# Query and key terms stored once in DRAM and repeated by the loads, with the projection chains in another order

## The chip, the cores and the metric

The kernel runs on one core of one Trainium2 chip. The metric is the device time of one execution in microseconds (us), as the median of several runs. The kernel before takes 1933.05 us (median of three runs, 1928.44 to 1935.05). The engines are called PE (TensorE, matmuls), PEld (its weight loads), DVE (VectorE), ACT (ScalarE), POOL (GpSimd) and SP (SyncE, which issues every DMA of this kernel). `L310` is line 310 of the kernel before, unless the text says that it is of the kernel after.

## The reference, cut to what matters

```
x: 2048 x 576;  q, k, v = x @ wq, x @ wk, x @ wv    (32 heads of 18, 4 segments of 512 positions)
for each segment s:
    p     = softmax(q_s k_s^T * 18**-0.5 + causal mask);   a_dot = p @ v_s
    a_mem = phi(q_s) M / (phi(q_s) z + 1e-6)               (phi(t) = t + 1 if t > 0 else exp(t))
    o_s   = g * a_mem + (1 - g) * a_dot                    (g = sigmoid(beta), one number a head)
    M, z += phi(k_s)^T v_s, sum of phi(k_s)
a = concat(o) @ wo
b = (silu(x @ w_gate) * (x @ w_up)) @ w_down               (hidden size 4608)
out = sg * a + (1 - sg) * b                                (sg = sigmoid of x . gate_w, one number a row)
```

All inputs and the output are f32. The kernel gets close to f32 by splitting each number into a high part and remainders, and multiplying the parts.

## The kernel before, in words

PE's program has three parts, one after the other in time.

**Part 1, the four segments (0 to 265 us).** A segment has nine *chains* and then eight *value steps*. A chain (`qk`, L301) is 14 matmuls (L127) into one PSUM bank and yields 128 rows of q or of k, transposed, for 512 positions; chain (m, u) is row block m of q (u = 0) or of k (u = 1), and chain (4, 0) holds the last 64 rows of both. The order is q0, k0, q1, k1, q2, k2, q3, k3, (4, 0). After the matmuls the bank is emptied: ACT copies the first bf16 term (L308), DVE takes the remainder `qr` (L309), ACT copies the second term (L318), POOL subtracts for the third (L319). The three terms stand in a tile `q3` of two buffers; `qr` has one. Where phi is wanted, ACT makes Relu and Exp of the bank (L316, L317) and DVE ends it (L321) into a tile `ph`. What a chain wants done besides is run in its middle (`mid`): in segment 0 the splitting of later weights (`q_split`, `v_split`, L104 on ACT and L105 on DVE).

The stores of q3 to DRAM (`stk`) are put on a list and issued by `flush` (L297 to L299), at a chain all but one (all but four at the last). A value step (`v_step`, L339) is 14 matmuls (L127, with `vw`) for 128 positions and half of the heads, into one of three banks. ACT copies the result to f32 (L347) and to the first bf16 term (L348), DVE takes the remainder (L349), ACT and POOL make the second and third term (L352, L353). In the segments after the first a memory step (L417) follows each value step, and during the chains the state M is brought up to date with the last segment's k and v: transposes of phi(k) (L379, L382), their copy `kt` (L380, L383, L384), matmuls L371. Before each value step `flush()` issues every store that is left; then, step by step, one of five loads of x for the next segment (`x_load`, L170) is issued, and split a step later (L104, L105, and L142, L143 for the fifth).

The stack in DRAM is `stk[2, 4, 576, 6, 512]`: for each row of q and of k six bf16 rows. For q these are high, middle, low, high, middle, high; for k low, middle, high, middle, high, high. So the 108 rows of one head (18 times 6) multiply to the six products of q and k parts that matter. A chain's stores write three of the six; DMAs from DRAM to DRAM (`copies`, L329) write the other three: four a segment after value steps 1 to 4 (L543), and for the last segment sixteen smaller ones during the feed-forward (L943).

**Part 2, feed-forward and attention together (265 to about 1820 us).** The 36 column blocks f of the hidden layer are run for one half of the positions and then for the other, 72 times eight *ticks*. Each tick is one group of matmuls (L910, L916), and `beat` adds down-projection groups (L758) and steps of the attention (`att_gen`, L689). In the first half each f loads raw weights (`raw`, L196), makes seven operands out of them and stores those (`wc`, L239; `rc`, L242); in the second half it loads them again (`w_fetch`, L562 and L566) as soon as PE has freed a buffer. Down-projection weights are loaded in the first half (`draw`, L201), split (L850, L851), stored (`dc`, L740), and fetched in the second (`dw`, L745).

The attention goes by *units*: 64 units, each two heads of one segment, five steps a unit. The maxima of a unit are found first (`s_bank`, L595), its probabilities later (`t_bank`, L635). Unit u has two tiles out of four, `qst` and `kst`, each [128, 2 heads, 512]; `stack_load` (L178, issues L182) fills their 108 rows by two DMAs, one for q and one for k, both heads at once. It is called at step 2 of the unit before (L700). Row maxima go to DRAM at step 3 (L696, which waits for POOL) and come back as three more rows of `qst` at step 0 of the next unit (`row_load`, L185).

**Part 3 (from about 1820 us)** is the output projection.

The order of every engine's instructions is written out by hand (manual schedule): each engine takes them in that order, and SP too, so a DMA whose data or buffer is not ready holds up all DMAs behind it. A DMA counts on one of eight semaphores in turn, and so also waits for the one that used its semaphore before.

Of the kernel before, what the change touches and what calls it, by code (L numbers as in the profile page):

```python
# [12 lines left out]
F32 = mybir.dt.float32  # L13
# [42 lines left out]
def gated_mix(ctx, tc, xT, wf, wd, wv, wo, beta, cmask, ident, bmask, out):  # L56
# [108 lines left out]
    def staging():  # L165
        return x_slot(*next(turns), F32).rearrange("p a b -> p (a b)")
# [92 lines left out]
    with ExitStack() as st:  # L259
# [22 lines left out]

        def v_load(hf):
            n = 288 + 2 * hf
            for a, b in ((0, 3), (3, 5)):
                raws["v", hf, a] = staging()[:, :(b - a) * n].rearrange("p (k n) -> p k n", n=n)
                nc.sync.dma_start(raws["v", hf, a], wv[:, a:b, 288 * hf:288 * hf + n])

        def v_split(hf):
            n = 288 + 2 * hf  # L290
            for a, b in ((0, 3), (3, 5)):
                split(vw[hf][:, 0, a:b, :n], vw[hf][:, 1, a:b, :n], raws["v", hf, a])

# [7 lines left out]
        def qk(s, m, u, mid=()):  # L301
            t = chain_tile()
            hi, lo = qw[m]
            products(t, w_stat(hi[:, u], lo[:, u]), x_side(*xs_of[s]))
            q3 = sp.tile([P, 3, L], BF, name="q3")
            qr = sp.tile([P, L], F32, name="qr", bufs=1)
            z0, z2 = (2, 0) if u else (0, 2)
            nc.scalar.activation(q3[:, z0], t, AF.Copy)  # L308
            nc.vector.tensor_sub(qr, t, q3[:, z0])  # L309
# [9 lines left out]
            nc.gpsimd.tensor_sub(q3[:, z2], qr, q3[:, 1])  # L319
            if ph is not None:  # L320
                nc.vector.scalar_tensor_tensor(ph, t, 0.0, ph, op0=OP.max, op1=OP.add)  # L321
            if m < 4:
                late.append((stk[u, s, m * P:m * P + P, 0:3], q3))
            else:
                late.append((stk[0, s, 512:D, 0:3], q3[0:64]))
                for z in range(3):
                    late.append((stk[1, s, 512:D, 2 - z], q3[64:128, z]))

        def copies(s, n=1):  # L329
            r = []  # L330
            for kind in range(2):
                for c, m in ((3, 2), (5, 1)):
                    z = 3 - m if kind else 0
                    for i in range(n):
                        a, b = D // n * i, D // n * (i + 1)
                        r.append((stk[kind, s, a:b, c:c + m], stk[kind, s, a:b, z:z + m]))
            return r

        def v_step(s, hf, i):  # L339
# [91 lines left out]
        for kt in range(NT):  # L431
# [4 lines left out]
            xr.append(raw)  # L436
        q_load(0, 1)
        nc.vector.memset(vf[:, :, :, DH:E], 1.0)
# [6 lines left out]
        for kt in range(NT):  # L445
            x_split(xs_of[0], kt, xr[kt])
        q_load(1, 0)
        q_load(1, 1)
        q_split(0, 1)
        q_split(1, 0)  # L450

        def small():
            nc.sync.dma_start(idt, ident)
            nc.sync.dma_start(bg, bass.AP(tensor=beta.tensor, offset=beta.offset, ap=[[0, P], [1, H]]))
            nc.scalar.activation(bg, bg, AF.Exp, scale=-1.0)
# [9 lines left out]

        loads = {0: [lambda: q_load(2, 0), lambda: q_load(2, 1)], 1: [lambda: q_load(3, 0), lambda: q_load(3, 1)],
                 2: [lambda: q_load(4, 0)], 4: [lambda: v_load(0)], 5: [lambda: v_load(1)], 7: [small]}
        def x_first():
# [18 lines left out]

        chains = [(m, u) for m in range(5) for u in range(2 if m < 4 else 1)]
        for s in range(NSEG):
            upd = upd_gen(s - 1) if s else None  # L490
            casts = []
            for n, (m, u) in enumerate(chains):
                mid = []
                if s == 0:
                    for z in loads.get(n, []):
                        z()
                    if n + 3 < 9:
                        mid.append(lambda n=n: q_split(*chains[n + 3]))
                    if n in (6, 7):
                        mid.append(lambda n=n: v_split(n - 6))  # L500
                if s == 1 and n < 3:
                    cast = masks(*((0, 3), (3, NT), (0, 0))[n])
                    casts.append(cast)
                if s == 1 and 3 <= n < 6:
                    mid.append(casts[n - 3])
                qk(s, m, u, mid)
# [11 lines left out]
            for n in range(8):  # L518
# [5 lines left out]
                if s < 3:  # L524
                    if n == 0:
                        xs_of[s + 1] = x_tiles(s + 1)
                    if n < 5:
                        raws["x", n] = x_load(s + 1, n)
                    if 1 <= n < 6:
                        x_split(xs_of[s + 1], n - 1, raws["x", n - 1])  # L530
                else:
# [7 lines left out]
                    for _ in range((0, 0, 0, 0, 3, 3, 6, 6)[n]):  # L539
                        if start[0][0] < 8:  # L540
                            start.pop(0)[1]()
                if 0 < n < 5 and s < 3:
                    nc.sync.dma_start(*copies(s)[n - 1])  # L543
        flush()


    with ExitStack() as st:
# [37 lines left out]
        stack_load(0)  # L585
        SPLAN = [[(0, 0, 3)], [(0, 1, 3)], [(384, 0, 0), (0, 0, 2)], [(384, 1, 0), (0, 1, 2)], [(0, 0, 1), (256, 1, 1)]]
# [102 lines left out]
        def att_gen():  # L689
            N = 10 * NB  # L690
            for tau in range(N + TL + VL + 4):
# [230 lines left out]
        for pos, (half, f) in enumerate(seq):  # L922
# [178 lines left out]
```

## Time and profile before

| what | before |
|---|---|
| median of three runs | 1933.05 us (1928.44 to 1935.05) |
| the profiled execution | 1932.2 us |
| its span, first to last instruction | 1930.4 us |
| PE busy | 1836.8 us (95%) |
| mean granted PE clock | 0.986 |
| DMA packets | 213860, 344.94 MB |
| segments start, on PE | 5.18, 65.03, 130.89, 201.01 us |
| their value steps start | 37.03, 106.06, 173.70, 242.64 us |
| first feed-forward matmul | 265.25 us |
| first s_bank of unit 0, of unit 32 | 292.7, 1109.4 us |

The profile is of one execution. Its *windows* give the busy time of each engine in a stretch, its *timeline* the instructions in order with the idle time before each and, behind an arrow, what ended that idle time; its *waits* sum these by line. Busy time of PE is that of pipelined matmuls, so a high share isn't full use, but idle time is idle.

### The profile page before, as it was taken

The page shows a single profiled execution, that of the slowest core. Times are in us where ns is not written, and L with a number is a line of the kernel's source. Part 1 is how long each engine was busy: PE and PEld are TensorE (multiplying, and loading weights), DVE is VectorE, ACT ScalarE, POOL GpSimd, SP SyncE. Part 2 cuts the span into 40 slices and gives each one's busy share as a digit, 9 for nine tenths or more (in the row PEclk, how much of TensorE's full clock was granted, in tenths as well). Part 3 has the DMA queues.
Part 4 walks back from the last instruction along what each step waited for, and adds up shares of the span by engine and source line. Part 5 has one row for each costly group of instructions (what it writes and reads, how often), then busy time and mean ns, then how long its engine had stood idle before and what let it go on. Part 6 is the DMA issues. An engine that isn't in the chain of part 4 may idle for free.

```text
span 1930.4 us, 35822 instructions
## 1 busy us (share of the span) xinstructions
PE 1836.8 (95%) x12508; PEld 1555.5 (81%) x12508; DVE 1229.5 (64%) x3032; ACT 965.2 (50%) x1800; POOL 857.6 (44%) x1246
## 2 busy tenths in 40 slices
PE   8888989999999999999998999999999999999999
PEld 6777878788788778877887788788888878888899
DVE  5354377767777787778767655656555666555355
ACT  6445454555664565566545545444544444455211
POOL 2222262345455555555554544544445444445121
PEclk9999989999999999999999999999999999999999
DMA  5553467745764674566456636544654465455544
GB/s 188 199 206 114 167 229 269 243 143 190 236 208 154 211 237 152 176 222 238 134 176 225 224 114 178 179 135 124 192 162 140 136 194 151 117 164 153 176 153 141
DMA packets 213860, 344.94 MB, mean 179 GB/s; under 512 B 37872, under 2 KB 100720, under 8 KB 213680
## 3 DMA queue, kind: packets, MB, share of 16 engines
q1 hardware_dynamic: 213680, 342.65, 54.5%
q8 instruction: 99, 1.62, 0.4%
q14 instruction: 81, 0.66, 0.1%
HBM read 208.49 MB, written 148.24 MB: 185 GB/s over the span
## 4 chain that ended last, share of the span: by engine, by line
PE 65%; DVE 8%; ACT 5%; DMA 4%; issue 3%; POOL 1%; SPq 0%; DVEq 0%; ACTq 0%; POOLq 0%
PE bank L910 25%; PE bank L758 23%; PE bank L916 4%; PE bank L635 3%; PE bank L595 3%; PE bank L127 3%; PE bank L664 2%; PE bank L666 1%; DMA raw<-in_wf_dram 1%; ACT L639 1%; DMA stk<-stk 1%; DVE p L712 1%; DMA woraw<-in_wo_dram 1%; ACT pe L639 1%; DVE hl L851 1%
## 5 line engine op out<-in xcount | busy, mean ns | idle before, releaser
L714 POOL TENSOR_TENSOR p<-pe,p 128x512 f16<-128x512 f32 x320 | 372.8, 1165 | 685.3 <-DVE p L712 603.5
L758 PE MATMUL bank<-dw,hh 128*128 128x288 f32 x2304 | 484.0, 303 | 16.4 <-DVE ya L763 11.9
L758 PEld LDWEIGHTS bank<-dw,hh 128*128 128x128 f32 x2304 | 379.9, 189 | 39.4 <-DVE ya L763 19.0
L639 ACT ACTIVATE pe<-bank 128x512 f32<-128x512 f32 x320 | 191.0, 597 | 340.7 <-PE bank L635 299.8
L758 PE MATMUL bank<-dw,hl 128*128 128x288 f32 x1152 | 341.2, 296 | 2.1 <-DVE hl L105 2.1
L763 DVE TENSOR_TENSOR ya<-bank,ya 128x288 f32<-128x288 f32 x352 | 159.9, 456 | 229.1 <-PE bank L758 227.0
L602 DVE CUSTOM_DVE_ANT_0 scr<-bank,cm 128x512 bf16<-128x512 f32 (+3 forms) x512 | 247.2, 483 | 15.6 <-PE bank L595 8.7
L758 PEld LDWEIGHTS bank<-dw,hl 128*128 128x128 f32 x1152 | 217.9, 189 | 2.5 <-DVE hl L105 2.5
L635 PE MATMUL bank<-qst,kst 111*128 111x512 bf16 (+3 forms) x512 | 151.8, 305 | 0.0
L712 DVE CAST p<-pe 128x512 f16<-128x512 f32 x320 | 151.0, 472 | 1.0 <-POOL pe L647 0.9
L647 POOL TENSOR_SCALAR_AFFINE_SELECT pe<-pe 128x256 f32<-128x256 f32 (+1 forms) x320 | 135.2, 422 | 11.2 <-ACT pe L639 10.2
L595 PE MATMUL bank<-kst,qst 108*128 108x512 bf16 (+3 forms) x512 | 126.3, 300 | 11.7 <-ACT pe L639 11.7
L993 DVE TENSOR_TENSOR bank<-bank,row 128x512 f32<-128x512 f32 x72 | 50.3, 699 | 106.0 <-ACT row L989 105.4
L980 ACT ACTIVATE row<-bank 128x512 f32<-128x512 f32 x72 | 43.0, 597 | 134.7 <-PE bank L916 134.0
L639 ACT ACT_TABLE_LOAD x66 | 84.7, 1283 | 46.3 <-PE bank L635 45.4
L105 DVE TENSOR_TENSOR hl<-row,hh 128x512 fp32r<-128x512 f32 x72 | 51.8, 720 | 76.4 <-ACT hh L104 76.4
L127 PE MATMUL bank<-xo,qhi 128*128 128x512 f32 x288 | 94.8, 410 | 5.3 <-ACT xo L104 5.2
L319 POOL TENSOR_TENSOR q<-qr,q 128x512 bf16<-128x512 f32 x36 | 42.3, 1175 | 118.6 <-ACT q L318 107.5
L635 PEld LDWEIGHTS <-kst 111*128 111x128 bf16 x512 | 47.9, 97 | 51.1 <-issue 35.9
L984 ACT ACTIVATE bank<-bank 128x512 f32<-128x512 f32 x72 | 41.9, 582 | 90.8 <-PE bank L910 87.2
L986 ACT ACT_TABLE_LOAD x67 | 86.0, 1283 | 1.2
L969 ACT ACTIVATE bank<-bank 128x512 f32<-128x512 f32 x72 | 42.0, 583 | 81.6 <-PE bank L910 71.5
(2083 smaller groups left out, 4286.9 us busy)
## 6 DMA issues: line engine op xcount, KB each, us to landing
raw<-in_wf_dram SPq DMA_DIRECT2D x72, 320.0 KB
dc<-dw SPq DMA_DIRECT2D x36, 576.0 KB
dw<-dc SPq DMA_DIRECT2D x36, 576.0 KB
qst<-stk SPq DMA_DIRECT2D x64, 216.0 KB
kst<-stk SPq DMA_DIRECT2D x64, 216.0 KB
stk<-q SPq DMA_DIRECT2D x32, 384.0 KB
draw<-in_wd_dram SPq DMA_DIRECT2D x36, 288.0 KB
vd<-vps SPq DMA_DIRECT2D x8, 912.0 KB
```

The lines of the kernel that those rows point to most:

```text
L127: nc.tensor.matmul(t, st[n], mv[n], start=(n == 0), stop=(n == 13))
L595: nc.tensor.matmul(t[:, c:c + w], qs[:KR, pr, P * i:P * i + P], ks[:KR, pr, 0:w], start=True, stop=True)
L602: nc.vector.tensor_tensor_reduce(scr[:, :w], t[:, c:c + w], cm[:, L - w:L], 1.0, -3.0e38, OP.add, OP.max, m[:, k:k + 1])
L635: nc.tensor.matmul(t[:, c:c + w], ks[:KR + 3, pr, P * j:P * j + P], qs[:KR + 3, pr, P * j:L], start=True, stop=True)
L639: nc.scalar.activation(pe, t, AF.Exp, scale=SCALE)
L647: nc.gpsimd.affine_select(d, d, pattern=pat, compare_op=OP.is_ge, fill=0.0, base=0, channel_multiplier=-1)
L712: nc.vector.tensor_copy(p1, pe)
L714: nc.gpsimd.tensor_sub(p2, pe, p1)
L758: nc.tensor.matmul(t, p, q[:, cs], start=(n == 0), stop=(n == 3 * CH - 1))
L763: nc.vector.tensor_add(ya[:, i, cs], t, ya[:, i, cs])
L910: nc.tensor.matmul(t, w[:, p, z], x[z][:, q], start=first and n == 0, stop=last and n == 5, skip_group_check=True)
L986: nc.scalar.activation(sg0, sg0, AF.Silu)
```

## The change

The stack in DRAM has three rows for each row of q or k, high, middle, low for both. A chain stores three terms at once, the last chain 64 rows to each of q and k; the copies from DRAM to DRAM are gone. `stack_load` now makes the six: for q the high rows three times over, the middle twice and the low once (a leading step of zero repeats the source), for k high, middle, low, then high, middle, then high. This takes ten DMAs a unit in place of two: six at step 2 (head 0's four, and the last 18 rows of q and of k for both heads) and four at step 3 (head 1), behind that step's store of maxima.

The chains go q0 to q3, (4, 0), k0 to k3. `q3` has four buffers and `qr` two, the phi of k one in place of two. `flush` keeps two stores back at every chain. The loads of x for the next segment are issued ahead of the last chains (segment 0: two, two and one ahead of chains 6, 7, 8; segments 1 and 2: one ahead of each of chains 4 to 8) and no more in the value steps. In segment 0 the splits of the value weights are spread over chains 3, 6, 7, 8, the f32 copy of the values is made by DVE and not by ACT, and the constants of beta are computed in segment 1's chain 7. The order of PE's instructions, by shapes and tiles, is that of before.

```diff
-    stk = dram.tile([2, NSEG, D, 6, L], BF, name="stk")
+    stk = dram.tile([2, NSEG, D, 3, L], BF, name="stk")
...
-    def stack_load(u):
+    def stack_load(u, pr):
         s, b = divmod(u, 16)
-        for kind, t in ((0, qst), (1, kst)):
-            src = stk[kind, s, 2 * b * DH:2 * b * DH + 2 * DH]
-            nc.sync.dma_start(t[u % NST][0:KR], src.rearrange("(j r) c n -> (r c) j n", r=DH))
+        q, k = (stk[kind, s, 2 * b * DH:2 * b * DH + 2 * DH].rearrange("(j r) z n -> r j z n", r=DH)
+                for kind in range(2))
+        tq, tk = qst[u % NST], kst[u % NST]
+        for z, n in ((0, 3), (1, 2)):
+            r0 = (0, 3 * DH)[z]
+            qz = q[:, pr, z]
+            nc.sync.dma_start(tq[r0:r0 + n * DH, pr],
+                              bass.AP(tensor=qz.tensor, offset=qz.offset, ap=[[0, n]] + list(qz.ap)))
+            nc.sync.dma_start(tk[r0:r0 + n * DH, pr], k[:, pr, 0:n].rearrange("r z n -> z r n"))
+        if pr == 0:
+            nc.sync.dma_start(tq[5 * DH:KR], q[:, :, 2])
+            nc.sync.dma_start(tk[5 * DH:KR], k[:, :, 0])
...
-            q3 = sp.tile([P, 3, L], BF, name="q3")
-            qr = sp.tile([P, L], F32, name="qr", bufs=1)
+            q3 = sp.tile([P, 3, L], BF, name="q3", bufs=4)
+            qr = sp.tile([P, L], F32, name="qr")
...
-                ph = sp.tile([P, L], F32, name=f"ph{m}{u}", bufs=2 if u or m == 4 else 1)
+                ph = sp.tile([P, L], F32, name=f"ph{m}{u}", bufs=2 if m == 4 else 1)
...
-            nc.scalar.activation(fv, pv, AF.Copy)
+            if s:
+                nc.scalar.activation(fv, pv, AF.Copy)
+            else:
+                nc.vector.tensor_copy(fv, pv)
...
+        chains = [(m, 0) for m in range(NT)] + [(m, 1) for m in range(4)]
...
-        chains = [(m, u) for m in range(5) for u in range(2 if m < 4 else 1)]
...
+                if s < 3:
+                    for kt in ((0, 1), (2, 3), (4,))[n - 6] if s == 0 and n > 5 else (n - 4,) if s and n > 3 else ():
+                        raws["x", kt] = x_load(s + 1, kt)
                 qk(s, m, u, mid)
-                flush(4 if m == 4 else 1)
+                flush(2)
...
-                    if n < 5:
-                        raws["x", n] = x_load(s + 1, n)
...
-                if 0 < n < 5 and s < 3:
-                    nc.sync.dma_start(*copies(s)[n - 1])
...
-                if n == 2 and u + 1 < 2 * NB:
-                    stack_load(u + 1)
+                if n in (2, 3) and u + 1 < 2 * NB:
+                    stack_load(u + 1, n - 2)
...
-            if half == 0 and 4 <= f < 20:
-                defer(4, lambda f=f: nc.sync.dma_start(*copies(NSEG - 1, 4)[f - 4]))
```

More of the change, by code (lines that the diff above doesn't have):

```diff
@@ L281, in q_split, with v_load, v_split @@
             split(qw[m][0][:, u], qw[m][1][:, u], raws[m, u])
-        def v_load(hf):
+        def v_load(hf, a, b):
             n = 288 + 2 * hf
[L285 to L289, printed above, removed]
+            raws["v", hf, a] = staging()[:, :(b - a) * n].rearrange("p (k n) -> p k n", n=n)
+            nc.sync.dma_start(raws["v", hf, a], wv[:, a:b, 288 * hf:288 * hf + n])
+        def v_split(hf, a, b):
             n = 288 + 2 * hf
-            for a, b in ((0, 3), (3, 5)):
-                split(vw[hf][:, 0, a:b, :n], vw[hf][:, 1, a:b, :n], raws["v", hf, a])
+            split(vw[hf][:, 0, a:b, :n], vw[hf][:, 1, a:b, :n], raws["v", hf, a])
         late = []
@@ L322, in qk @@
             if m < 4:
-                late.append((stk[u, s, m * P:m * P + P, 0:3], q3))
+                late.append((stk[u, s, m * P:m * P + P], q3))
             else:
[L325 to L337, printed above, removed]
+                for kind in range(2):
+                    late.append((stk[kind, s, 512:D], q3[64 * kind:64 * kind + 64]))
         def v_step(s, hf, i):
@@ L436, in gated_mix @@
             xr.append(raw)
-        q_load(0, 1)
+        chains = [(m, 0) for m in range(NT)] + [(m, 1) for m in range(4)]
+        q_load(*chains[1])
         nc.vector.memset(vf[:, :, :, DH:E], 1.0)
@@ L446, in gated_mix @@
             x_split(xs_of[0], kt, xr[kt])
[L447 to L450, printed above, removed]
+        q_load(*chains[2])
+        q_load(*chains[3])
+        q_split(*chains[1])
+        q_split(*chains[2])
         def small():
@@ L454, in small, with betas @@
             nc.sync.dma_start(bg, bass.AP(tensor=beta.tensor, offset=beta.offset, ap=[[0, P], [1, H]]))
+        def betas():
             nc.scalar.activation(bg, bg, AF.Exp, scale=-1.0)
@@ L498, in gated_mix @@
                         mid.append(lambda n=n: q_split(*chains[n + 3]))
-                    if n in (6, 7):
-                        mid.append(lambda n=n: v_split(n - 6))
+                    if n in halves:
+                        mid.append(lambda n=n: v_split(*halves[n]))
                 if s == 1 and n < 3:
@@ L584, in gated_mix @@
             nc.gpsimd.memset(mbs[i], 0.0)
-        stack_load(0)
+        for pr in range(2):
+            stack_load(0, pr)
         SPLAN = [[(0, 0, 3)], [(0, 1, 3)], [(384, 0, 0), (0, 0, 2)], [(384, 1, 0), (0, 1, 2)], [(0, 0, 1), (256, 1, 1)]]
```

17 lines of the change are left out of this document (11 added, 6 removed).

## The prediction

> **What bounds the kernel now.** I read first the page's busy shares, then the windows by stage. The program's first part (L127 projections, four segments of the sequence) ends at 265.25 us, where the first feed-forward matmul (L910) starts; feed-forward and attention fill the rest.
>
> ```profile
> PE 1836.8 (95%) x12508; PEld 1555.5 (81%) x12508; DVE 1229.5 (64%) x3032; ACT 965.2 (50%) x1800; POOL 857.6 (44%) x1246
> ```
>
> ```profile
> 0.00:65.03 65.03, 51.27 (x238) 43.83 (x239) 29.98 (x48) 38.12 (x70) 17.71 (x26) 0.93 0.64 220
> 65.03:130.89 65.86, 57.96 (x347) 51.52 (x347) 28.51 (x75) 34.10 (x70) 17.76 (x21) 1.00 0.48 172
> 130.89:201.01 70.12, 60.75 (x349) 54.18 (x348) 30.70 (x83) 34.22 (x70) 18.42 (x22) 0.95 0.46 165
> 201.01:265.25 64.24, 59.35 (x349) 52.90 (x348) 32.02 (x82) 32.33 (x67) 27.43 (x28) 0.97 0.47 173
> 265.25:292.70 27.45, 20.33 (x66) 14.58 (x65) 19.46 (x42) 15.39 (x37) 16.12 (x19) 0.69 0.64 225
> 292.70:1109.40 816.70, 783.78 (x5283) 652.51 (x5283) 613.79 (x1480) 462.00 (x908) 411.47 (x591) 0.99 0.60 201
> 1109.40:1782.50 673.10, 663.63 (x4912) 554.44 (x4911) 400.41 (x1079) 318.86 (x513) 321.98 (x508) 1.00 0.52 153
> ```
>
> Each row: stretch, length, busy time of PE, PEld, DVE, ACT, POOL, then granted clock, DMA share, GB/s. From 292.7 us on PE is busy 96 to 99%: nothing there can be won by moving loads. The four segments leave PE idle 36 of 265 us. PE's, ACT's and SP's timelines of the first segment say why.
>
> ```profile
> 46.75 3.25 PE L127 MATMUL bank<-vw,xo 128*128 128x288 f32 x12 [3.98 <-DVE r L349]
> 54.15 1.87 PE L127 MATMUL bank<-vw,xo 128*128 128x290 f32 x12 [1.09 <-DVE r L349]
> 61.82 2.93 PE L127 MATMUL bank<-vw,xo 128*128 128x290 f32 x12 [3.31 <-DVE gl L351]
> ```
>
> ```profile
> 34.51 0.60 ACT L308 ACTIVATE q<-bank 128x512 bf16<-128x512 f32 x1 [2.06 <-DMA stk<-q]
> ...
> 52.31 0.63 ACT L104 ACTIVATE xo<-xo 128x512 fp32r<-128x512 f32 x1 [3.54 <-DMA xo<-in_xT_dram]
> ...
> 59.81 0.63 ACT L104 ACTIVATE xo<-xo 128x512 fp32r<-128x512 f32 x1 [3.02 <-DMA xo<-in_xT_dram]
> ```
>
> ```profile
> 38.73 10.55 SPq L299 DMA_DIRECT2D stk<-q x6
> 49.38 1.03 SPq L170 DMA_DIRECT2D xo<-in_xT_dram x2
> 50.50 0.53 SPq L543 DMA_DIRECT2D stk<-stk x1
> ```
>
> PE waits for PSUM banks that ACT and DVE have not emptied. ACT is late twice: in the chains it waits for a store to free one of two q3 buffers, and in the value steps for x loads. Those stand on SP behind the stores of the last chains, and on the rings behind the 576 and 1152 KB copies. The same x waits come in segment 1 (ACT: 4.60, 1.51, 4.25 us) and segment 2 (4.81, 1.55, 4.64); the last makes the first state update of the next segment late (L371 waits 2.91, 3.96, 2.77 us for ACT's kt). After such waits the trace's clock records show half speed (6.8 us from 45.1, 3.4 us each at 62.2, 147.5, 191.9, 215.8).
>
> **The change, part by part.** PE's instruction list keeps shapes and order, so only waits move.
>
> *Segment 0.* Chains stay at 31.85 us: their loads keep their lead, and ACT per chain is at most copy 0.60, split 0.66 to 0.95, Relu and Exp 1.23, second copy 0.61, some 3.2 us against PE's 3.18. The 28.0 us of value steps (37.03 to 65.03) become eight times 1.87 (PE's step where nothing waits) plus 1 for ACT's lag: 16. ACT's step falls to 0.41 + 0.46 + 0.61 and a 0.5 wait for DVE, below 2.0, since the vf copy (0.39) goes to DVE, which has 0.46 + 0.46 + 0.69 a step. The x loads, issued from chain 6 on (26 us), take 5 to 10 us and are there at 37. Gain **12**.
>
> *Segments 1 and 2.* Segment 1's chains take 41.03 - 1.46 - 2.91 = 36.7 without waits, its value steps 24.83 - 2.92 - 0.61 = 21.3. I leave 0.5 for the kt wait (ACT needs 4.4 us from a chain's end to kt, PE comes after 4.0) and 0.2 more: 58.7 each, against 65.86 and 70.12. Gains **7.2** and **11.4** (in segment 2 two spells of half clock go too).
>
> *Segment 3.* Chains 41.63 become 37.2; its value steps lose only L417's 0.45 us wait. Gain **4.8**. The transition (265 to 293) waits on feed-forward operands being made (L229) and keeps its length.
>
> At nothing: the second head's loads move past the maxima store, which waits for POOL (L696, 89.1 us in all); from that store to their first use were 9.7 us or more. The 28 copies leave SP (0.49 to 0.63 us each) and the rings; where they ran in the feed-forward PE did not wait for them. One buffer for each k phi is enough, as the transposes end at chain 4 and the first k chain is 5; if they ran late, ACT would wait for one of them (0.3 us). The gate constants move to segment 1's chain 7, ahead of their first reader. The late stores keep two behind: with four q3 buffers a store may take 12.7 us after its chain, and POOL (about 5), issue and landing need some 8.
>
> *Ten stack loads for two.* This costs. SP: 8 more issues a unit. The nearest rows are the old stack load (0.36 and 0.41) and the v fetch (L189, 0.54, whose two sides differ in form as these do); I take 0.54, near 4.5 us a unit of 19.8 in the second half. Behind them on SP stand weight fetches (L562), maxima (L696) and row loads (L185). Each DMA also waits for the one eight before it, through eight semaphores. Rings: in the trace an old stack load of 108 rows ends with 13 completion marks, the 8-row maxima store with 9, the 3-row load with 4, every 128-row one with 16; so few rows use few engines, one for each mark but one. The new loads lead with 3 and 2 on the DRAM side and I expect 4 and 3 marks. A 1 KB packet takes 46 ns (median). If all use the same engines, the two busiest get 8 x 18 + 2 x 4 = 152 packets a unit, 7.0 us, against 36 and 1.7 before. The second half's DMA share of 0.52, less the old stack loads' 0.06, is 0.46 of other traffic; 7.0 of 19.8 us is 0.35 more: 0.81, not full. A load right behind the first head's six is issued 4 x 0.6 + 2 x 0.45 - 0.8 = 2.5 us later than before and finds about 1 us more on the ring: 3.5 us later; behind all ten, some 5.
>
> [...]
>
> Who waits? I paired landings with first uses. Old stack loads land 3.8 us or more before use, median 10. Weight fetches of the second half: 24 of 312 have under 5 us, and 5 us on every one would come 18.6 us short in all; about a third stand behind a burst: 5 us. Of 36 down-weight loads (L201), 24 are short-notice; 13 of these have under 3.5 us; a quarter stand behind a burst, some 1.8 us short each, half of it on PE: 3 us. Bounds: nothing (slack takes all) and 60 us (every weight fetch 6 us late comes 58.8 short). I take **8**, near the lower end, since a burst lasts 3 to 6 us and most slack is longer; the first unit's ten loads, issued near 280 us with 7.5 us of slack before, are in it.
>
> Sum: -12 - 7.2 - 11.4 - 4.8 + 8 = -27.4 on the profiled execution's 1932.2 us (span 1930.4 and 1.8 around it): 1904.8. The median of the runs is 0.85 above that execution: **1905.7**.
>
> **The rivals.**
>
> *Nothing paid later* (1898): slack hides all bursts. For: no matmul has waited more than 0.5 us in all for a stack load. Against: 0.02 to 3.5 us slack of many L201 loads.
>
> *Half the gain* (1923): x comes early, but the kt waits (L371, 9.6 us) and the L417 waits (7.7) are ACT's and DVE's own and stay: 17.3 less. For: ACT's 4.4 us from chain to kt is already more than PE's 4.0. Against: segment 3's value steps, with operand splits but no x loads, run at 22.6 for 21.2.
>
> *The narrow loads take over* (slower, 1950): weight fetches of the second half land later than their slack. The shortfalls summed over all fetches pass 41 us (the gain and the 0.3%) when each is 5.6 us later; at 6 they are 59. With 59 the sum is 1933 - 35.4 + 59 = 1957; I put it at 1950, some stalls covering others. For: 0.81 is a mean, and stretches at 0.69 DMA share (275 to 350) reach 0.95; two bursts within 3 us, in about 13 of the second half's units, make 11 DMAs in a row. Against: the first-half fetch slack is 11 us or more (L196), and a fetch far behind a burst loses nothing.
>
> That the chains' reorder does nothing by itself is part of the second rival.
>
> **How the numbers follow.** Forecast 0.55, nothing paid 0.17, half the gain 0.14, narrow loads take over 0.14. Within 0.3% of 1933 (1927 to 1939, about what a measurement of this kernel can tell from no change) I see 0.05, from the seams of the last two; faster by more 0.84, slower 0.11. The range leaves out most of the last rival: 1893 (no tax and 4 us more from the clock) to 1930 (tax of 32).
>
> **What would show it.** Right: the first L910 near 230 us; no ACT wait for in_xT in segments 1 to 3; L371 and L417 waits near 1 us; stack loads with 4 and 3 marks, issue about 0.5 us. Tax: PE waits in the feed-forward for L201's ACT copy, for wo from DMA, or for kst; their sum is to be near 8. Wrong: the first L910 after 245, or PE's waits for DMA over 30.

## The result, and the profile after

The changed kernel takes **1913.1 us** (median of four runs, 1911.2 to 1916.0), beside 1932.65 us of the kernel before on the same chip: a ratio of 0.9902, with a 95% interval of 0.988 to 0.9925. That is 19.6 us faster. The forecast was 1905.7, 7.4 us too low. The profiled execution took 1915.99 us (span 1914.2), the highest of its four. In this part line numbers are those of the kernel that the fence is from; L917, L602 and L369 of the changed kernel are the old L910, L595 and L371.

The page of the changed kernel has this line of busy times. PE does the same 12508 matmuls. Its busy time is nearly the same in sum, but the windows below show that this is two shifts that cancel.

```profile
PE 1834.5 (96%) x12508; PEld 1552.9 (81%) x12508; DVE 1231.5 (64%) x3040; ACT 965.6 (50%) x1792; POOL 858.2 (45%) x1246
```

The windows of the changed kernel, cut at the same instructions as those of before (four segments, the transition to unit 0's first maxima, the rest of the first half, most of the second half); the columns are as in the prediction.

```profile
0.00:54.12 54.12, 46.45 (x238) 40.00 (x239) 31.26 (x49) 35.88 (x61) 17.07 (x25) 1.00 0.63 217
54.12:115.60 61.48, 58.54 (x348) 52.62 (x347) 33.17 (x90) 36.96 (x77) 19.18 (x22) 0.97 0.38 134
115.60:173.32 57.72, 57.09 (x349) 51.41 (x348) 30.85 (x83) 34.47 (x71) 18.50 (x22) 1.00 0.38 138
173.32:231.12 57.80, 57.13 (x349) 51.40 (x348) 29.83 (x75) 31.00 (x62) 26.73 (x27) 1.00 0.46 169
231.12:263.10 31.98, 19.62 (x66) 13.62 (x64) 19.70 (x42) 15.51 (x37) 16.09 (x19) 0.77 0.52 185
263.10:1091.65 828.55, 790.30 (x5283) 656.87 (x5282) 610.61 (x1480) 462.19 (x908) 410.89 (x591) 0.98 0.58 193
1091.65:1766.38 674.73, 664.33 (x4912) 554.19 (x4911) 401.28 (x1079) 319.31 (x513) 322.50 (x508) 1.00 0.50 155
```

Set beside the old lengths, each row is a term of the prediction's sum:

| stretch | before | after | gain | predicted |
|---|---|---|---|---|
| segment 0 | 65.03 | 54.12 | 10.9 | 12 |
| segment 1 | 65.86 | 61.48 | 4.4 | 7.2 |
| segment 2 | 70.12 | 57.72 | 12.4 | 11.4 |
| segment 3 | 64.24 | 57.80 | 6.4 | 4.8 |
| transition | 27.45 | 31.98 | -4.5 | |
| first half after it | 816.70 | 828.55 | -11.9 | |
| second half | 673.10 | 674.73 | -1.6 | |
| end | 147.90 | 147.82 | 0.1 | |
| transition to end | 1665.15 | 1683.08 | -17.9 | -8 |

Part 1 gained 34.1 of the 35.4 us forecast. The tax on the rest was 17.9 us in this execution and not 8: 11.9 in the first half, 4.5 in the transition, 1.6 in the second half. By medians the tax is about 34.1 - 19.6 = 14.5 us, an estimate that takes part 1 to be as long in the other executions (this one was 2.9 us above the median).

Not all of this is waiting. In part 1 PE's busy time falls from 229.3 to 219.2 us and its idle time from 35.9 to 11.9: 24.0 of the 34.1 us are waits, and 10.1 are matmuls that take less time. Before, the clock records show half speed for 20.5 us of part 1, in five spells; now for 3.4 us, in one. In the first half it is the other way round: busy 790.30 us for 783.78, so 6.5 of the 11.9 us are longer matmuls and 5.3 are waits.

In segments 2 and 3 PE is idle 0.63 and 0.67 us now (length less busy time). Segments 0 and 1 show what stayed. This is PE's timeline of the changed kernel; the bracket is the idle time before the instruction and what ended it.

```profile
45.64 1.85 PE L127 MATMUL bank<-vw,xo 128*128 128x290 f32 x12 [0.19 <-DVE r L347]
48.88 1.85 PE L127 MATMUL bank<-vw,xo 128*128 128x290 f32 x12 [1.11 <-DVE r L347]
52.16 1.85 PE L127 MATMUL bank<-vw,xo 128*128 128x290 f32 x12 [1.17 <-DVE gl L349]
...
67.69 2.52 PE L369 MATMUL bank<-vf,kt 128*128 128x152 f32 x9 [2.89 <-ACT kt L378]
```

ACT's and DVE's timelines of the same stretch give the reason: ACT hardly waits for x loads any more (0.4 us in all), but for DVE.

```profile
44.51 0.43 ACT L346 ACTIVATE vps<-bank 128x288 bf16<-128x288 f32 x1 [1.25 <-DVE vf L345]
45.53 0.46 ACT L350 ACTIVATE vps<-r 128x288 bf16<-128x288 f32 x1 [0.59 <-DVE r L347]
45.88 0.61 ACT L104 ACTIVATE xo<-xo 128x512 fp32r<-128x512 f32 x1
47.74 0.43 ACT L346 ACTIVATE vps<-bank 128x288 bf16<-128x288 f32 x1 [1.25 <-DVE vf L345]
```

```profile
43.29 0.82 DVE L105 TENSOR_TENSOR xo<-xo,xo 128x512 fp32r<-128x512 f32 x1 [1.03 <-ACT xo L104]
44.03 0.45 DVE L345 COPY vf<-bank 128x288 f32<-128x288 f32 x1
45.04 0.46 DVE L347 TENSOR_TENSOR r<-bank,vps 128x288 f32<-128x288 f32 x1 [0.56 <-ACT vps L346]
```

The two engines pass one chain between them: ACT's split of x (0.61), DVE's half of it (0.82), DVE's copy of the values (0.45), ACT's first term (0.43), DVE's remainder (0.46), ACT's second term (0.46), and again ACT's split. The sum is 3.23 us, and so is ACT's step (44.51 to 47.74); the short gaps and overlaps between the six cancel.

The tax begins in the transition. SP's, then ACT's, then PE's timeline of the changed kernel (in SP's, the time is that of the issue):

```profile
245.57 0.84 SPq L186 DMA_DIRECT2D qst<-stk  x1
246.68 0.72 SPq L188 DMA_DIRECT2D kst<-stk  x1
...
252.46 0.61 SPq L198 DMA_DIRECT2D v<-vd  x1
253.12 0.62 SPq L210 DMA_DIRECT2D draw<-in_wd_dram  x1
254.11 0.34 SPq L248 DMA_DIRECT2D wc<-wo__2470  x1
```

```profile
259.42 0.42 ACT L235 ACTIVATE wo__2630<-ws 128x256 fp32r<-128x256 f32 x1 [5.33 <-DMA wc<-wo__2470]
```

```profile
261.04 2.26 PE L917 MATMUL bank<-xo,wo__2614 128*128 128x512 f32 x6 [4.50 <-DVE row L1002]
```

Unit 0's ten loads hold SP for 6.9 us; behind them stands the store of an operand, whose tile ACT needs again. ACT waits 5.33 us for its landing, DVE behind ACT, and PE 4.50 us for DVE. Later in the first half the same happens at a smaller scale. SP, ACT and PE, 630 us on:

```profile
877.25 0.61 SPq L188 DMA_DIRECT2D kst<-stk  x1
877.97 0.35 SPq L248 DMA_DIRECT2D wc<-wo__10997  x1
```

```profile
883.50 0.42 ACT L235 ACTIVATE wo__11127<-ws 128x256 fp32r<-128x256 f32 x1 [2.77 <-DMA wc<-wo__10997]
```

```profile
886.08 0.38 PE L602 MATMUL bank<-kst,qst 108*128 108x512 bf16 x1 [1.56 <-ACT pe L646]
```

This store was issued right behind a unit's loads. Its sixteen completion marks came from 1.86 to 5.43 us after the issue: some early, the last late. In the nine-engine kernel below, whose PE order is the same, the same store has its marks from 1.92 to 2.11 us after the issue, ACT waits 0.2 us for it, and PE does not wait at this matmul.

The longer matmuls of the first half stand mostly in spells of half clock, and a spell does not follow from the length of a wait alone. Here is one wait of PE, first in the change, then with nine engines, and behind it the window that follows it in each (the third figure from the end is the granted clock):

```profile
486.17 0.38 PE L602 MATMUL bank<-kst,qst 108*128 108x128 bf16 x2 [2.07 <-ACT pe L646]
```

```profile
484.27 0.38 PE L602 MATMUL bank<-kst,qst 108*128 108x128 bf16 x2 [2.08 <-ACT pe L646]
```

```profile
487.10:490.50 3.40, 3.40 (x13) 3.09 (x12) 2.75 (x9) 1.02 (x3) 2.91 (x4) 0.51 0.54 176
```

```profile
484.97:488.37 3.40, 3.40 (x24) 3.24 (x23) 3.37 (x9) 1.26 (x4) 2.90 (x5) 1.00 0.46 156
```

The first half of the change has 16 PE waits of over 1 us and seven spells (487.1, 558.7, 753.3, 893.2, 961.5, 1022.9 and 1036.6 us, 3.4 us each); with nine engines there are 12 such waits and three spells, before 12 and four. In the clock records of an execution all spells start a multiple of 3.413 us apart. On this grid the wait of 2.07 us lies within one step, the one of 2.08 us on two (about 1.5 and 0.6 us). But with nine engines a wait of 1.75 us at 349.6 lies within one step too, and no spell follows: the traces give no rule, and no run tests one.

Against the nine-engine kernel the changed one falls back at nine places between 330 and 1062 us, by 0.4 to 2.1 us each and 12.6 together (starts of the same matmuls set side by side). Four of the nine hold a spell that nine engines do not have (487.1, 753.3, 961.5, 1036.6). Three more kernels below have the same ten loads, and their first half took 827.63 us (first loads later), 823.88 (change, values on ACT) and 822.03 (x late): it is 5.3 to 11.9 us longer than before, and this execution of the change is the worst of the four.

### The profile page after: what moved, and what is told of

Read it like the earlier page. It is cut to its first block, busy times and chain, and to the rows that moved or that the text cites. A ratio compares the mean times of both kernels' runs of the same rounds, so it can differ in the third digit from the quotient of the medians.

```text
span 1914.2 us, 36563 instructions
## 1 busy us (share of the span) xinstructions
PE 1834.5 (96%) x12508; PEld 1552.9 (81%) x12508; DVE 1231.5 (64%) x3040; ACT 965.6 (50%) x1792; POOL 858.2 (45%) x1246
## 2 busy tenths in 40 slices
DMA packets 204457, 330.83 MB, mean 173 GB/s; under 512 B 38192, under 2 KB 95664, under 8 KB 204272
## 4 chain that ended last, share of the span: by engine, by line
PE 76%; ACT 6%; DVE 6%; DMA 5%; issue 4%; POOL 2%; SPq 2%; ACTq 0%; DVEq 0%; POOLq 0%
PE bank L917 26%; PE bank L765 23%; PE bank L127 10%; PE bank L923 5%; PE bank L642 3%; PE bank L602 3%; PE bank L671 2%; PE bank L673 1%; ACT L646 1%; DMA draw<-in_wd_dram 1%; PE bank L369 1%; ACT pe L646 1%; ACT L991 1%; ACT hh L104 1%; PE bank L415 0%
## 5 line engine op out<-in xcount | busy, mean ns | idle before, releaser
L765 PEld LDWEIGHTS bank<-dw,hh 128*128 128x128 f32 x2304 | 380.8, 190 | 40.4 <-DVE ya L770 20.5
L654 POOL TENSOR_SCALAR_AFFINE_SELECT pe<-pe 128x256 f32<-128x256 f32 (+1 forms) x320 | 136.2, 426 | 13.5 <-ACT pe L646 12.1
L602 PE MATMUL bank<-kst,qst 108*128 108x512 bf16 (+3 forms) x512 | 126.6, 301 | 13.8 <-ACT pe L646 13.3
```

The source lines that it names most:

```text
L602: nc.tensor.matmul(t[:, c:c + w], qs[:KR, pr, P * i:P * i + P], ks[:KR, pr, 0:w], start=True, stop=True)
L654: nc.gpsimd.affine_select(d, d, pattern=pat, compare_op=OP.is_ge, fill=0.0, base=0, channel_multiplier=-1)
L765: nc.tensor.matmul(t, p, q[:, cs], start=(n == 0), stop=(n == 3 * CH - 1))
```

## The experiments

*Theories.* **Rings**: the ten narrow loads of a unit put their rows on two, three or nine of the sixteen DMA engines, and a store or fetch that has rows on all sixteen ends with the slowest. (No record names an engine. The numbers are the completion marks, 3, 4 and 10, less one, and the packet records agree. In the change, six stretches of 1 KB packets hold a unit's four narrow loads of 3 and 2 in the lead and nothing else, and three packets go at a time; in eight of nine that also hold the two loads of 18 rows it is nine. Before, where a unit's two loads ended with 13 marks, it is 12 in 27 of 33.) **Issue**: the ten issues hold SP, and what is queued behind comes later. For part 1, the prediction's theory was that x loads behind stores and copies made ACT late; what was open is which of the edits frees them. Each kernel was timed beside the kernel before on its own chip (medians of that between 1932.5 and 1935.9), so ratios are compared.

| kernel | median us | ratio, 95% interval |
|---|---|---|
| the change | 1913.1 | 0.9902 (0.988 to 0.9925) |
| nine engines | 1904.1 | 0.9847 (0.9829 to 0.9866) |
| six rows stored | 1898.7 | 0.9822 (0.9804 to 0.984) |
| before, x early | 1905.4 | 0.9855 (0.9833 to 0.9877) |
| x late | 1916.4 | 0.9912 (0.9896 to 0.9927) |
| first loads later | 1909.6 | 0.9854 (0.9833 to 0.9876) |
| issue alone | 1899.9 | 0.9821 (0.9801 to 0.9841) |
| values on ACT | **1891.4** | 0.9768 (0.9752 to 0.9783) |
| two engines alone | 1907.3 | 0.9852 (0.9838 to 0.9867) |
| change, values on ACT | 1907.6 | 0.9866 (0.9844 to 0.9888) |
| three undone | 1893.7 | 0.9794 (0.9774 to 0.9813) |
| spread alone | 1899.5 | 0.9824 (0.9805 to 0.9842) |

**Nine engines.** The change, with the repeated rows in another order of the tile, so that the DMAs lead with the 18 rows and not with the 3 or 2 copies.

```diff
-  ap=[[0, n]] + list(qz.ap)
+  ap=[qz.ap[0], [0, n]] + list(qz.ap[1:])
-  k[:, pr, 0:n].rearrange("r z n -> z r n")
+  k[:, pr, 0:n]
```

> The changed kernel with the stack's rows in another order (row by row, its terms side by side, for q and k alike, so that the sums of products are the same). The ten loads a unit stay, but lead with 18 rows in place of 3 or 2, so each should end with 10 completion marks. Issue theory (part 2 pays because SP spends near 0.7 us on each of ten issues and what stands behind them is late): the time stays near the changed kernel's 1913, at most 3 us under it, since one k load in five a unit may get cheaper to issue. Ring theory (part 2 pays because the loads crowd on two or three engines): most of the 14 to 17 us that part 2 lost come back, near 1900.

Measured: 1904.1. All ten loads end with 10 marks now, where eight of them had 4 or 3, and these eight land in 2.2 to 2.4 us where they took 3.9 to 4.2 (medians by line). Windows of this kernel, from its first feed-forward matmul:

```profile
231.19:261.99 30.80, 19.13 (x65) 13.35 (x64) 19.70 (x42) 14.97 (x36) 16.05 (x19) 0.78 0.50 180
261.99:1078.44 816.45, 783.64 (x5282) 652.32 (x5282) 611.02 (x1480) 463.44 (x909) 412.40 (x591) 0.99 0.59 196
1078.44:1751.55 673.11, 663.65 (x4912) 554.35 (x4911) 400.53 (x1079) 319.29 (x513) 322.53 (x508) 1.00 0.50 155
```

The first half is back at 816.45 us (before: 816.70), and the second at 673.11 (673.10). Yet SP spends more on the ten issues than in the change: 413 us summed over the trace against 390. So of the two theories, rings; 9 us by medians, 14.3 by the two profiled executions (1914.2 to 1899.9). Of the 12.1 us that the first half gains, 5.4 are waits and 6.7 the longer matmuls. The transition, 30.80, is not mended.

**Six rows stored.** The change, with the stack as before (six rows a row, two loads a unit), but the other three rows made by the chains' stores (three DMAs a chain with a repeated source) and not by copies.

```diff
-    stk = dram.tile([2, NSEG, D, 3, L], BF, name="stk")
+    stk = dram.tile([2, NSEG, D, 6, L], BF, name="stk")
...
+  if kind:
+      return [(d[:, 0:3], t), (d[:, 3:5], t[:, 0:2]), (d[:, 5], t[:, 0])]
```

> The changed kernel with the stack of six rows in DRAM and two loads a unit as before, but the six rows written by the chains' own stores (three stores a chain from the tile of terms, some repeating a row), so still no copy from DRAM to DRAM. Both theories of the stack loads (issue and ring): part 1 keeps its 33 us, part 2 returns to its length of before, 1900 +- 3. Rival (part 2 is longer because it starts at another phase or with other data late, whatever the stack loads): it stays at 1910 to 1914.

Measured: 1898.7, as expected. First feed-forward matmul at 232.5, so part 1 keeps the gain though it stores twice as much; transition 26.86, first half 816.63, second 673.27. Nothing of the tax is left when two loads a unit take the place of the ten: the ten loads are all of it.

**Before, x early.** The kernel before with one edit: the x loads ahead of the last chains.

```diff
+                if s < 3:
+                    for kt in ((0, 1), (2, 3), (4,))[n - 6] if s == 0 and n > 5 else (n - 4,) if s and n > 3 else ():
+                        raws["x", kt] = x_load(s + 1, kt)
...
-                    if n < 5:
-                        raws["x", n] = x_load(s + 1, n)
```

> The kernel before with one edit: the x loads of the next segment are issued ahead of the last chains as in the change; copies, two q3 buffers, chain order and stack loads are of before. Theory that x behind the stores on SP is the cause of part 1's waits: about 25 of the 33 us of part 1 come (segment 0 less, as ACT still waits for q3), no tax in part 2: 1908 +- 4. Rival (the q3 buffers and the copies on the rings make ACT late): 8 to 10 us, near 1924.

**X late.** The change with that edit taken back.

> The changed kernel with one edit taken back: x loads stand in the value steps again, behind all stores of the chains. Theory that the place of the x loads is the main cause: ACT waits for x again in three segments, 15 to 25 us lost, 1928 to 1938. Rival (without copies on the rings x comes in time from there too): under 6 us lost, 1913 to 1919.

These two go together. Before with x early: 1905.4, its first feed-forward matmul at 240.45, so this one edit takes 24.8 us off part 1 and beats the whole change. The change without it: 1916.4, first feed-forward matmul at 234.16; only 3 us lost: the theory's 1928 to 1938 **missed**, its rival's 1913 to 1919 held. ACT's waits for x in the kernel before, in before with x early, and in the change with x late say why; the columns are us in all, times, longest.

```profile
ACT xo L104 <- DMA xo<-in_xT_dram: 20.2, 7, 4.8
ACT xs L142 <- DMA xo<-in_xT_dram: 12.8, 3, 4.6
```

```profile
ACT xo L104 <- DMA xo<-in_xT_dram: 1.4, 2, 1.2
```

```profile
ACT xo L104 <- DMA xo<-in_xT_dram: 5.9, 5, 1.7
ACT xs L142 <- DMA xo<-in_xT_dram: 3.8, 2, 1.9
```

33.0 us of waiting fall to 1.4 when the loads go early, and to 9.7 when they stay where they were but the copies are gone and q3 has four buffers (those two, and the other edits of part 1, are not told apart). The two cures overlap: 24.8 us by the one, 31.1 by the other, 34.1 together.

**First loads later.** The change with unit 0's loads at ticks 4 and 6 of the first column block.

```diff
-        for pr in range(2):
-            stack_load(0, pr)
...
+        for pr in range(2):
+            defer(4 + 2 * pr, lambda pr=pr: stack_load(0, pr))
```

> The kernel after, with unit 0's ten stack loads put into the eight ticks of the first column block (six at tick 4, four at tick 6) and not ahead of the first raw weight loads. The trace of after loses about 6.6 us against before between 255 and 330 us, beginning with a wait of PE of 4.50 us at 261 behind an operand store that waited for SP. If the burst of ten issues at that place is what makes the first operands late, some 3 to 6 us come back: about 1909 (1907 to 1911), and the wait at 261 is gone. Rival: the first unit's place does not matter, since what is late there is the weights that all share the rings; then 1912 to 1914 as after, with the wait moved to another line.

Measured: 1909.6. The wait of 4.50 us at 261 is gone, in its place PE waits for the loads themselves:

```profile
260.07 0.38 PE L600 MATMUL bank<-kst,qst 108*128 108x512 bf16 x1 [1.40 <-DMA kst<-stk]
```

The transition is 28.31 us, 3.7 shorter than in the change; the first half stays at 827.63. By ratios the gain is 9.3 with an uncertainty of 6 either way, which holds 3.7.

**Issue alone** and **two engines alone** put one suspect each into the six-row kernel, in loads that nobody uses: eight small loads of the repeated form a unit (many issues, 1/32 of the bytes), or two large ones whose leading step is 2 (few issues, many bytes on few engines). **Spread alone** has the large loads with the same bytes, each row twice in a row. (The edits are cut to the line that matters.)

```diff
+  nc.sync.dma_start(dum[0][0:n * DH, c:c + 16], bass.AP(tensor=a.tensor, offset=a.offset, ap=[[0, n]] + list(a.ap)))
```

```diff
+  nc.sync.dma_start(dum[u % 4, pr, 0:2 * n], bass.AP(tensor=a.tensor, offset=a.offset, ap=[[0, 2]] + list(a.ap)))
```

```diff
-  ap=[[0, 2]] + list(a.ap)
+  ap=[a.ap[0], [0, 2], a.ap[1]]
```

> The kernel with six stored rows, no copies and two stack loads a unit (1898.7 us) and, in addition, eight small loads a unit of the repeated form (rows of 32 bytes) at the places where the change has its ten; the tile that they fill is used by nobody. So SP issues ten loads a unit as in the change, but the bytes of the small ones are 1/32. Theory that the time of SP's issues is the tax: 64 units x 8 issues x about 0.65 us is 333 us more of SP, and what is queued behind is late as in after: 1903 to 1912. Rival, that the narrow loads' bytes on two or three DMA engines are the tax: 1898 to 1901, no more than 2 us lost.

> The kernel with six stored rows and two stack loads a unit (1898.7 us) with two loads more a unit, of 88 and 128 rows of 1 KB whose leading step repeats the source twice, from DRAM to a scratch of their own in DRAM: few issues (128 in all), but their rows go to two DMA engines each. Theory that piling bytes on a few engines is the tax: about 108 rows on each of two engines a unit, near what the ten loads put on their busiest ones, so most of the loss of after comes back: 1906 to 1915. Rival, that the issues on SP are the tax: 128 issues of 0.7 us cost no more than 0 to 2 us: 1898 to 1901.

> The kernel with six stored rows and the two extra loads a unit of 88 and 128 rows of 1 KB, with the same bytes in an order that spreads them: each row is written twice in a row, so the leading steps are 44 and 64 and not 2. It tells whether the 5.9 to 9 us that the extra loads cost were the place of their bytes or the bytes themselves. Theory, the place: 1898 to 1902. Rival, 14 MB more traffic costs the same wherever it goes: 1905 to 1909.

Measured against 0.9822 of the six-row kernel: issue alone 0.9821, so 341 us more of SP cost nothing in the median. One of its four runs, the profiled one, took 1906.1: it lost 6.9 us between 246 and 286 us, where unit 0's loads stand, so there SP's time may bite; the other three took 1899.7 to 1900.1 and lost nothing of the kind. Two engines alone 0.9852 (1907.3), spread 0.9824 (1899.5): the same bytes cost 5.4 us (uncertain by 4.5), by medians 7.9, when they lie on two engines, as read from the marks, and nothing that shows when spread. The extra loads ended with 3 marks in the one, with 12 and 16 in the other. First half of "two engines alone", then of "spread alone":

```profile
260.41:1083.22 822.81, 785.08 (x5283) 652.02 (x5282) 609.97 (x1480) 462.52 (x909) 410.43 (x591) 0.99 0.61 204
```

```profile
259.76:1076.46 816.70, 783.41 (x5282) 652.68 (x5281) 612.29 (x1480) 462.90 (x909) 411.22 (x591) 0.99 0.62 206
```

6.1 us, 4.4 of it idle time of PE, at a DMA share that is if anything higher in the faster one (0.62). The marks of other DMAs point to the way. From 262 us on, the median time between the first and the last mark of an operand store is 0.82 us before, 1.28 in the change, 0.66 with nine engines, 1.47 with two engines alone, 0.83 spread; the last mark comes at 3.67, 4.18, 3.39, 4.50 and 3.60 us. A second way is not told apart from this one: a DMA that lands late also holds its semaphore, and SP waits for it before it issues what stands behind. (In the traces of before and of the change every eighth DMA has the same semaphore, and none of the 1355 and 1831 was issued ahead of the last mark of the DMA eight before it; 49 and 203 were issued within 0.3 us after that mark.) In the first half SP waited 20.9 us for stack and extra loads with two engines alone and 1.5 with spread alone; 12.1 in the change and not at all with nine engines.

**Values on ACT**, in the six-row kernel and in the change: the f32 copy of segment 0's values goes back to ACT.

```diff
-            if s:
-                nc.scalar.activation(fv, pv, AF.Copy)
-            else:
-                nc.vector.tensor_copy(fv, pv)
+            nc.scalar.activation(fv, pv, AF.Copy)
```

> The kernel with six stored rows, no copies and two stack loads a unit (1898.7 us), with the f32 copy of the values in segment 0 made by ACT as before and not by DVE. Theory: in after, ACT waits 1.24 us a value step for that DVE copy, so segment 0's value steps took 18.2 us where 16 were expected, and the transposed keys of segment 1 came 2.89 us late; putting it back gives 2 to 5 us: 1894 to 1897. Rival: DVE's copy relieved ACT as it was meant to, and putting it back costs as much as it gives: 1898 to 1901.

> The change whole, with one of its edits undone: the f32 copy of the values in segment 0 is made by ACT again and not by DVE. With six stored rows this edit gave about 10 us (1898.7 to 1891.4 on two chips, ratios 0.9822 and 0.9768). Theory: it is a cost of its own, 3 us in segment 0's value steps and 3.5 in segment 1, whose transposed keys are not late any more: 1903 to 1908. Rival: it gives only with the two wide stack loads, since with the narrow ones ACT is behind their loads anyway: 1911 to 1914.

Measured: 1891.4 in the six-row kernel, 10.4 us by ratios (uncertain by 4.6) and 7.3 by medians, more than the 2 to 5 expected; 1907.6 in the change, 7.0 by ratios (uncertain by 6.1). ACT's timeline of the six-row kernel with the values on ACT:

```profile
42.97 0.39 ACT L339 ACTIVATE vf<-bank 128x288 f32<-128x288 f32 x1
43.27 0.42 ACT L340 ACTIVATE vps<-bank 128x288 bf16<-128x288 f32 x1
44.30 0.46 ACT L344 ACTIVATE vps<-r 128x288 bf16<-128x288 f32 x1 [0.62 <-DVE r L341]
44.66 0.61 ACT L104 ACTIVATE xo<-xo 128x512 fp32r<-128x512 f32 x1
45.18 0.40 ACT L339 ACTIVATE vf<-bank 128x288 f32<-128x288 f32 x1
```

ACT has one more copy in a step and a step of 2.21 us in place of 3.23, since it goes from its split of x straight on and DVE's half of that split has left the chain. Segment 0's value steps take 15.0 us (35.92 to 50.91) for 18.2; the wait for `kt` in segment 1 falls from 2.92 to 1.35 us. The first feed-forward matmul comes 8.0 us earlier (224.55 for 232.51), in the change 6.1 (224.99 for 231.12). The rest of the 10 lies in the transition (0.6 shorter) and the first half (3.1 shorter); why the first half gains is not settled.

**Three undone.** The change with ten loads a unit kept, but rows in the spread order, unit 0's loads later and the values on ACT.

> The change with its ten loads a unit, but the three suspected costs undone together: destination rows in the order of the stored rows (the loads end on more engines), unit 0's loads inside the first column block, the values of segment 0 copied by ACT. Theory that the three add: 1913.1 less 9 (rows), less 4 (first loads, by the trace), less 7 (values): 1893 (1890 to 1897). Rival, that they cover one another, as late x loads and the copies did: 1898 to 1904.

Measured: 1893.7, the value of the sum. Windows of this kernel:

```profile
225.03:252.32 27.29, 18.89 (x65) 13.37 (x64) 19.98 (x43) 15.94 (x38) 16.11 (x19) 0.75 0.52 184
252.32:1069.26 816.94, 781.84 (x5282) 650.01 (x5282) 612.18 (x1480) 461.90 (x907) 411.38 (x591) 1.00 0.60 197
1069.26:1742.40 673.14, 663.70 (x4911) 554.38 (x4911) 400.90 (x1079) 319.14 (x513) 322.46 (x508) 1.00 0.51 155
```

All three stretches are those of before within 0.3 us. So these three make up the tax and the shortfall of part 1, and they add, as far as an uncertainty of about 6 us on each can tell. Both this kernel and the six-row one with values on ACT (1891.4, the best) beat the change and the kernel before.

## Why the prediction was right, and where its terms failed

The direction and the mechanism held, and the sum of part 1 came out, in part by luck; the term that was mis-sized is **the tax of the ten loads**: 8 us predicted, 17.9 in the profiled execution, 14.5 by medians.

- *Only waits move.* Right for the instructions (12508 matmuls) and not for the time. Busy time fell by 10.1 us in part 1 and rose by 6.5 in the first half, mostly as spells of half clock went and came; that the sums agree (1834.5 us for 1836.8) is chance. The prediction named spells of part 1 that would go, and put nothing for spells that the tax would bring.
- *Part 1, 35.4 us.* Measured 34.1, first feed-forward matmul at 231.12 for "near 230". ACT's waits for x fell from 33.0 us to 0.4, as forecast. That the sum is so near is luck: segment 0's value steps came out 2.2 us and segment 1 2.8 longer than forecast, segment 0's chains 1.0 and segments 2 and 3 2.6 shorter. And the terms are right with a reason that is only half of the cause: the early loads are sufficient (24.8 us alone) and not necessary (without them 31.1 remain).
- *Value steps of segment 0, 16 us.* Measured 18.2. The step that failed is "ACT's step falls ... below 2.0, since the vf copy (0.39) goes to DVE". It added up each engine's own work and one handoff. The copy moved to DVE stood behind DVE's half of the split of x and ahead of ACT's first term, and closed a chain of six instructions, 3.23 us a step.
- *Segment 1, 7.2 us.* Measured 4.4: of the `kt` wait 2.89 us stayed where 0.5 was left for it. Putting the copy back shortens it to 1.39, so ACT's lag of segment 0 is half of it. Behind the wait stands a spell of half clock (3.4 us from 67.2), which the forecast did not have and which is gone with the copy put back. Segments 2 and 3 came out 1.0 and 1.6 us better than forecast, with no `kt` wait at all.
- *Issues of 0.54 us.* Too low: 0.71 and 0.66 for the repeated and transposed loads (median), 6.1 us a unit where 4.5 was taken (390 us over 64 units). It made no difference that the medians show: 341 us of extra issues cost nothing in the six-row kernel.
- *4 and 3 marks, the rows on the same engines.* The marks are right, and rows on few engines are the tax: 9 us by medians came back when all ten loads ended with 10 marks. Whether it is always the same engines no run tells, so the 7.0 us a unit on the two busiest stay the author's estimate. The price was worked out from pairs of landing and first use of *loads*: 5 us for the second half's weight fetches and 3 for the first half's down-weight loads. The second half lost 1.6 us. The first half lost 11.9, and the waits in it and in the transition go in part through *stores*: an operand's tile is free only when its store has landed, and ACT waits for that (5.33, 2.77, 2.2 and 2.2 us at four stores; 4.7, 0.2, 1.1 and 0.2 at the same four with nine engines; before, 1.4 at one) and for L210's loads (5.8 us in all; with nine engines 1.9, before 0.3). The prediction had "half of it on PE: 3 us" for these loads and nothing for stores. A store's last mark came only 0.5 us later in the median; it is the few behind a burst that count. And over half of what the first half lost, 6.5 us, is longer matmuls, mostly at half clock, for which the prediction had nothing. As the first half differs by 6.5 us between kernels with the same loads, some of the 17.9 may be chance.
- *The transition keeps its length.* Wrong by 4.5 us, of which 3.7 are where unit 0's ten loads stand. "In it", the prediction said of them, without a price.
- *Rivals.* "Nothing paid later" fell, as 14.5 us were paid; "narrow loads take over" had the right mechanism and too high a price and the wrong half; "half the gain" fell, as ACT's lag went with the x waits in segments 2 and 3.

What stays open: which of the nine places in the first half goes back to a late store, which to an L210 load and which to something else, and why a spell of half clock follows a wait in one kernel and not the same wait in another. The waits of ACT alone do not tell: "three undone" has 5.4 us of them for L210's loads and 3.7 for one store, and loses nothing.

## What to carry to other kernels

Before a DMA is split or its source repeated, count the marks with which it ends: here 14 MB in loads that ended with 3 marks cost 7.9 us by medians at a mean DMA share of 0.61 in the first half, and under 1 us in loads that ended with 12 and 16. When slack is worked out, pair stores with the reuse of their buffer too, not only loads with their first use. And when a copy is moved to an idle engine, follow the chain that it joins: an engine with time to spare can still be the longer way round (a step of 3.23 us here, 2.21 with the copy put back). Last, split a gain or a loss into idle and busy time of PE before it is put down to waits: here 10.1 of 34.1 us and 6.5 of 11.9 us were not waits but shorter or longer matmuls.

## What the runs showed of the hardware

- Fewer bytes can cost more: the change moves 330.83 MB for 344.94 and its loads are the tax, 14.5 us by medians; 14 MB more, spread, cost under 1 us (1899.5 for 1898.7).
- The marks of a DMA follow the number of leading rows: 2 gave 3 marks, 3 gave 4, 8 gave 9, 18 gave 10, 44 gave 12, 64 gave 16.
- Issues on SP, medians by line: loads whose two sides differ in form took 0.71 (repeated), 0.66 (transposed) and 0.59 us (the v fetch) in the change, and the v fetch 0.54 before; the change's raw loads, operand stores and operand fetches took 0.34 to 0.43.
- Half clock in the records, summed over an execution: 57.8 us before, 53.7 in the change, 27.6 in the six-row kernel, 20.2 in the best one (up to 2.3 us of each behind the last instruction). Within the span, the spells before and in the change last 3.4, 6.8, 13.7 or 17.1 us. One of 3.4 us costs up to 1.7 us beside the wait ahead of it, by an estimate from the window at 487.1 us: 13 matmuls at a clock of 0.51, where the same 3.40 us with nine engines hold 24 at 1.00. But only seven spells stand behind the 16 PE waits of over 1 us in the change's first half.
